# Windowed attention with a gated feed-forward on one core: constants built elsewhere, and a new list for the order of the work

## The chip, the cores and the metric

The kernel runs on one core of a Trainium2 chip. A core has five engines that run beside each other and wait for one another by semaphores: TensorE (PE, matrix products; PEld is its weight load), VectorE (DVE), ScalarE (ACT), GpSimd (POOL) and SyncE (SP), whose queue starts the transfers here. The metric is the device time of one launch in microseconds (us); lower is better.

## The reference

Eight batches, eight heads, 576 positions, 64 per head. Each query sees itself and the 127 positions before it, with a bias that falls with distance by a slope of the head:

```python
scores = scale * np.matmul(q, k.transpose(0, 1, 3, 2))
slopes = 2.0 ** (-8.0 * (np.arange(H) + 1) / H)
mask = (rel >= 0) & (rel < window)             # rel = query position - key position, window = 128
scores = np.where(mask, scores - slopes * np.abs(rel), -1e9)
attn = softmax(scores);  x = attn @ v          # heads side by side: x is (8, 576, 512)
h = gelu(x @ w_in);  u, v = halves of h        # w_in: 512 x 1024
v_n = (v - mean(v)) / sqrt(var(v) + 1e-6) * g_ln
gated = u * (w_sg @ v_n + b_sg)                # w_sg: 576 x 576, over positions
out = x + gated @ w_out
```

## The kernel before

The core works through 32 pairs of heads (pair n is batch n // 4) and, for each batch, the feed-forward part on all 576 positions. A position block is 64 wide (`R`), a tile 128 (`P`). Products of the feed-forward part are made from a high and a low half of every operand (three products for one).

**The order of the work is written out by hand.** Every step has a name and one engine. `ORDER` (line 1141) lists all of them; each engine runs its own steps strictly in the order of the list, and waits at a step until what it needs is there. The steps that matter here, n being the pair, b the batch and t the tile:

- SyncE: `q` load queries and keys, `L` load values, `i` load 128 rows of a weight matrix (0 to 7: `w_in`, 8 to 11: `w_out`), `wl` and `tl` load `w_sg`. The weights come into four buffers with the tag `g`.
- TensorE: `a`, `c` scores of a pair in two parts (`*` is both), `t`, `T` transpose the probabilities (four products each), `z` the first block's, `V` the product with the values, `w` and `v` the gate's part of `x @ w_in` for a tile, `tt` the same for the last 64 positions, `u` the other half of `x @ w_in` (two steps of 12 products for each of four column blocks), `y` the product with `w_sg` (eight steps of 14 products), `O` the product with `w_out`. `W` are idle products on a tile of zeros; they compute nothing that is used. `W0` has 12 of them, `W1` four.
- VectorE: `A`, `B`, `C`, `G` add the bias and take the row's extreme, `R` reciprocal of the sums, `X`, `Y` mask the transposed probabilities on their way out of PSUM, `2` adds up a pair's result, `m`, `b`, `o` and the odd `-` steps split weights into halves, `n..b`, `n..c`, `vn`, `tj`, `tn` normalise the gate (`tn0` is the last such step that batch 0 needs ahead of its `y` steps), `gm` multiplies by the gate, `Us`, `Ul` sums of weights.
- ScalarE: `e`, `E`, `f`, `F`, `j` exponentials, `d`, `H` weight splitting, `P`, `p`, `x`, `h`, `k` copies, `vg`, `tg`, `ug` the gelu, and for the first four pairs the scaling `s`, `r`.
- GpSimd: `S` (and later `s`, `r`) scaling, `+` and the even `-` weight splitting, `l` low halves, `w-`, `t-`, `n..p`.

Ahead of the list stand the constants, lines 85 to 156: an identity for the transposes (`ident`), two triangular masks side by side for both halves of the partitions (`m_both`, used by `X` and `Y`), a selection mask (`sel`, used by `A`) and four bias tables, one for each pair of a batch (`biases`, used by `A` to `G`). They need small temporaries (`ones`, `lo`, `sel_f`, `rel_i`, `rel`), which the kernel before takes from the tag `g`. ScalarE makes the masks' halves and all 16 parts of the bias tables (line 152). In the list before, the `y` steps of batch 0 begin with `y030`.

## Time and profile before

| | before |
|---|---|
| median of 3 runs | 595.48 us (595.41 to 596.38) |
| the profiled execution | 595.18 us |
| its span, first to last instruction | 593.5 us |
| TensorE busy | 567.6 us (96%) |
| VectorE busy | 485.4 us (82%) |
| ScalarE busy | 383.9 us (65%) |
| GpSimd busy | 295.5 us (50%) |

The profile shows one execution. Busy time counts instructions that run, from the start to the end of each. The chain of waits follows the work back from the last instruction, at each step to what released it; its pieces don't overlap, so that they can be added. Two lines of the page, the busy share of TensorE and VectorE in 40 equal slices in tenths, show where the span is not full:

```
PE   6778799799999999999999999999999999999997
DVE  5999898799897978799887896888787989676647
```

### The profile page before, as it was taken

Reading aid. Unit: us, or ns where it says so; the run is one execution under the profiler, and the core shown is the slowest. Engines: PE = TensorE matmul, PEld = TensorE weight load, DVE = VectorE, ACT = ScalarE, POOL = GpSimd, SP = SyncE. Lnnn points to the kernel's source line nnn. Section 1 sums busy time; section 2 is a strip of 40 time slices with the busy share of each in tenths; the row PEclk is TensorE's granted clock in tenths of the full one; section 3 lists DMA queues with packets and bytes.
Section 4 is the critical chain, followed back from the end, with each engine's and each line's share of the span. In section 5 each row is a group of like instructions: output and inputs, shape, how many; then the busy total and the mean of one; then the engine's idle time right before and its main releaser. Section 6 shows DMA issues by size and latency. Waiting matters only on the chain.

```text
span 593.5 us, 14592 instructions
## 1 busy us (share of the span) xinstructions
PE 567.6 (96%) x5495; PEld 513.5 (87%) x5495; DVE 485.4 (82%) x1332; ACT 383.9 (65%) x1085; POOL 295.5 (50%) x283
## 2 busy tenths in 40 slices
...
DVE  5999898799897978799887896888787989676647
...
GB/s 280 172 255 113 150 94 64 7 116 133 121 168 1 200 93 26 183 46 222 164 159 23 140 150 113 122 1 304 113 127 65 37 193 170 2 11 157 127 2 80
DMA packets 43561, 69.78 MB, mean 118 GB/s; under 512 B 3554, under 2 KB 31202, under 8 KB 43492
## 3 DMA queue, kind: packets, MB, share of 16 engines
...
q14 instruction: 26, 0.21, 0.1%
HBM read 56.27 MB, written 12.58 MB: 116 GB/s over the span
## 4 chain that ended last, share of the span: by engine, by line
PE 83%; DVE 11%; ACT 4%; issue 1%; POOL 1%; DVEq 0%; POOLq 0%; ACTq 0%
PE ps_m L602 12%; PE ps_m L1051 12%; PE ps_m L900 11%; PE ps_m L604 11%; PE ps_m L603 11%; PE ps_a L343 4%; PE ps_m L380 3%; PE ps_a L276 3%; PE ps_s L276 3%; PE ps_s L380 3%; DVE e L293 2%; PE ps_m L936 1%; PE ps_m L935 1%; DVE tmp L213 1%; ACT e L309 1%; DVE px L352 1%
## 5 line engine op out<-in xcount | busy, mean ns | idle before, releaser
L330 POOL TENSOR_TENSOR e<-e,rr 128x512 f32<-128x512 f32 (+1 forms) x88 | 78.6, 911 | 127.5 <-DVE rr L321 85.8
L309 ACT ACTIVATE e<-e,stats 128x128 f32<-128x128 f32 (+1 forms) x288 | 110.8, 388 | 15.2 <-DVE stats L293 14.8
L352 DVE TENSOR_TENSOR px<-ps_a,m_both 128x1024 f32<-128x1024 f32 x64 | 77.3, 1213 | 8.5 <-PE ps_a L343 8.5
L602 PE MATMUL ps_m<-ws,region 128*128 128x288 f32 x256 | 78.5, 307 | 0.0
L604 PE MATMUL ps_m<-ws,region 128*128 128x288 f32 x256 | 75.8, 296 | 0.0
L603 PE MATMUL ps_m<-ws,region 128*128 128x288 f32 x256 | 75.7, 296 | 0.0
L725 POOL TENSOR_TENSOR rs<-rs,mhalf 128x1 f32<-128x1 f32 (+1 forms) x40 | 30.7, 769 | 64.5 <-DVE rs L722 60.6
L309 ACT ACTIVATION_READ_ACCUMULATOR e<-e,stats 128x1 f32 x288 | 54.8, 190 | 0.0
L1007 POOL TENSOR_TENSOR region<-u,region 128x576 fp32r<-128x576 f32 x28 | 42.7, 1530 | 23.4 <-ACT region L1001 19.9
L400 POOL TENSOR_TENSOR xs<-xf,xs 128x576 fp32r<-128x576 f32 x32 | 47.0, 1475 | 13.8 <-ACT xs L397 13.8
L1001 ACT ACTIVATE region<-u 128x576 fp32r<-128x576 f32 x35 | 23.8, 685 | 42.8 <-PE ps_m L603 18.7
L343 PE MATMUL ps_a<-ident,e 128*128 128x128 f32 x256 | 40.9, 282 | 9.5 <-issue 3.7
L602 PEld LDWEIGHTS ps_m<-ws,region 128*128 128x128 f32 x256 | 48.4, 189 | 1.6 <-issue 0.8
L604 PEld LDWEIGHTS ps_m<-ws,region 128*128 128x128 f32 x256 | 48.2, 188 | 0.4 <-DVE region L737 0.2
L603 PEld LDWEIGHTS ps_m<-ws,region 128*128 128x128 f32 x256 | 48.3, 189 | 0.1
L602 PE MATMUL ps_m<-wi,xs 128*128 128x512 f32 x112 | 46.8, 418 | 0.0
L603 PE MATMUL ps_m<-wi,xs 128*128 128x512 f32 x112 | 44.3, 395 | 0.0
L604 PE MATMUL ps_m<-wi,xs 128*128 128x512 f32 x112 | 44.2, 395 | 0.0
L343 PEld LDWEIGHTS ps_a<-ident,e 128*128 128x128 f32 x256 | 30.7, 143 | 14.8 <-issue 5.6
L941 DVE TENSOR_TENSOR u<-ps_m,u 128x576 f32<-128x576 f32 x32 | 23.9, 751 | 18.8 <-PE ps_m L936 11.4
L1058 DVE TENSOR_TENSOR xf<-ps_m,xf 128x576 f32<-128x576 f32 x48 | 35.8, 750 | 4.1 <-PE ps_m L1051 3.9
L293 DVE CUSTOM_DVE_ANT_0 e<-ps_s,bias 128x128 f32<-128x128 f32 (+1 forms) x140 | 34.9, 286 | 2.6
(215 smaller groups left out, 1651.3 us busy)
## 6 DMA issues: line engine op xcount, KB each, us to landing
...
```

The lines of the kernel that those rows point to most:

```text
L293: nc.vector.tensor_tensor_reduce(out=dst, in0=src, in1=bs, scale=-1.0 / math.sqrt(D), scalar=3e38, op0=ALU.add, op1=ALU.min, accum_out=acc)
L309: nc.scalar.activation(x, x, AF.Exp, bias=self.nm[0:n, i:i + 1], scale=-1.0, accum_out=self.sm[0:n, i:i + 1])
L330: nc.gpsimd.tensor_tensor(x, y, self.rr[0:n, i:i + k].rearrange("p (m o) -> p m o", o=1).broadcast_to([n, m, c]), ALU.mult)
L343: burst([lambda t=t: nc.tensor.transpose(cv[:, t // 2, t % 2], self.pr[j][:, t, :].rearrange("p (h c) -> p h c", h=2), ident[:, j * R:j * ...
L352: nc.vector.tensor_tensor(xv, cv, mv, ALU.mult)
L400: nc.gpsimd.tensor_tensor(lo_of(self.xs), self.xf, hi_of(self.xs).bitcast(F32), ALU.subtract)
L602: nc.tensor.matmul(dst, ah, bh, start=(first and i == 0), stop=False)
L603: nc.tensor.matmul(dst, ah, bl, start=False, stop=False)
L604: nc.tensor.matmul(dst, al, bh, start=False, stop=(last and i == n - 1))
L900: nc.tensor.matmul(dst, left(n, g, c)[:, ms], right(n, h, c), start=first and c == 0 and k == 0, stop=c == 1 and k == 2, skip_group_check= ...
L1007: engine.tensor_tensor(lo, u(n)[:, fs], hi[:, fs].bitcast(F32), ALU.subtract)
L1051: nc.tensor.matmul(dst, p, q, start=first and f == 0 and k == 0, stop=f == 1 and k == 2, skip_group_check=True)
```

## The change

The constants' temporaries move into one tile with the tag `px`, the buffer in which `X` and `Y` later write the masked probabilities. The four bias tables are made by VectorE, one operation of 128 x 448 each, from a table `rel` in which the slope ratio of the two heads is multiplied in beforehand. `m_both` is cut by four GpSimd selections in place, and the second half of `ident` is copied by GpSimd. The tile of zeros is filled first. With the tag `g` free from the start, the list can place the first loads one behind another. `ORDER` is a new list of the same steps; its idle product ahead of the first scores is `W1` in place of `W0`, and the `y` steps of batch 0 begin with `y000`. Below, the diff of the constants in full, and of the list the part up to the first `y` steps.

```diff
@@ -87,71 +87,59 @@
 
     warm = const.tile([P, 1], F32, name="warm")
     nc.scalar.activation(warm, mhalf, AF.Exp)
-    ident = const.tile([P, P + P // 2], F32, name="ident")
-    make_identity(nc, ident[:, 0:P])
-    nc.vector.tensor_copy(ident[:, P:P + P // 2], ident[:, 0:P // 2])
+    spare = const.tile([P, S2], F32R, name="spare")
+    nc.vector.memset(spare.bitcast(F32), 0.0)
 
 
     def halves(name, n, dt=F32):
         return const.tile([P, n], dt, name=name)
 
-    def twice(x):
-        nc.scalar.copy(x[R:P], x[0:R])
-
-    def temp(name, dt=F32):
-        return mlp.tile([P, P], dt, name=name, tag="g", bufs=NF)[0:R, 0:R]
-
-    ones = temp("ones")
+    setup = att.tile([P, 2 * T * 2 * P], F32, name="setup", tag="px", bufs=1)
+    ones, sel_f, rel_i = [setup[0:R, i * R:(i + 1) * R] for i in range(3)]
+    rel = setup[:, 4 * R:11 * R]
+    low, high = slice(0, R), slice(R, P)
     nc.vector.memset(ones, 1.0)
-
-
-    m_both = halves("m_both", 2 * P)
-    nc.vector.memset(m_both, 1.0)
-    lo = temp("lo")
-    nc.gpsimd.affine_select(out=lo, in_=ones, pattern=[[1, R]], compare_op=ALU.is_ge, fill=0.0, base=0, channel_multiplier=-1)
-    spare = const.tile([P, S2], F32R, name="spare")
-    nc.vector.memset(spare.bitcast(F32), 0.0)
-    for i in range(2):
-        hs = slice(i * R, (i + 1) * R)
-        nc.scalar.activation(m_both[hs, i * R:(i + 1) * R], lo, AF.Copy, scale=-1.0, bias=1.0)
-        nc.scalar.copy(m_both[hs, P + i * R:P + (i + 1) * R], lo)
-
-    sel_f = temp("sel_f")
     nc.gpsimd.affine_select(out=sel_f, in_=ones, pattern=[[1, R]], compare_op=ALU.is_gt, fill=0.0, base=0, channel_multiplier=-1)
-    sel = halves("sel", 4 * R, U8)
-    nc.vector.memset(sel[:, 0:R], 1)
-    for j in range(2):
-        hs = slice(j * R, (j + 1) * R)
-        for i in range(2):
-            nc.scalar.copy(sel[hs, (2 * i + 1) * R:(2 * i + 2) * R], sel_f)
-        nc.scalar.activation(sel[hs, 2 * R:3 * R], sel_f, AF.Copy, scale=-1.0, bias=1.0)
-    sel_first, sel = [sel[:, i * 2 * R:(i + 1) * 2 * R].rearrange("p (t c) -> p t c", t=2) for i in range(2)]
+    nc.gpsimd.iota(rel_i.bitcast(I32), pattern=[[-1, R]], base=0, channel_multiplier=1)
 
 
     slopes = [2.0 ** (-8.0 * (h + 1) / H) for h in range(H)]
     assert all(math.frexp(x)[0] == 0.5 for x in slopes) and D == 4 ** 3
-    rel_i = temp("rel_i", I32)
-    nc.gpsimd.iota(rel_i, pattern=[[-1, R]], base=0, channel_multiplier=1)
-    rel = mlp.tile([P, 4 * R], F32, name="rel", tag="g", bufs=NF)
-    alone, merged, plain = [rel[0:R, i * R:(i + 1) * R] for i in (0, 1, 2)]
-    nc.vector.tensor_copy(merged, rel_i)
+    alone, merged, plain = [rel[low, i * R:(i + 1) * R] for i in (0, 1, 2)]
+    nc.vector.tensor_copy(merged, rel_i.bitcast(I32))
     nc.vector.tensor_scalar(plain, merged, float(R), None, ALU.add)
     nc.vector.scalar_tensor_tensor(out=merged, in0=sel_f, scalar=float(P), in1=merged, op0=ALU.mult, op1=ALU.add)
     nc.vector.scalar_tensor_tensor(out=alone, in0=sel_f, scalar=1e9 / min(slopes), in1=merged, op0=ALU.mult, op1=ALU.add)
-    nc.scalar.copy(rel[0:R, 3 * R:4 * R], merged)
-    nc.scalar.copy(rel[R:P], rel[0:R])
-
+    nc.vector.tensor_copy(rel[low, 3 * R:4 * R], merged)
+    nc.scalar.activation(rel[high, 0:4 * R], rel[low, 0:4 * R], AF.Copy, scale=slopes[1] / slopes[0])
+    nc.scalar.copy(rel[high, 4 * R:7 * R], rel[low, R:4 * R])
+    nc.vector.tensor_scalar(rel[low, 4 * R:7 * R], rel[low, R:4 * R], slopes[1] / slopes[0], None, ALU.mult)
+
+    sel = halves("sel", 4 * R, U8)
+    nc.vector.memset(sel[:, 0:R], 1)
+    for hs in (low, high):
+        nc.scalar.copy(sel[hs].rearrange("p (t c) -> p t c", t=2)[:, :, R:2 * R], over(sel_f, 2))
+        nc.scalar.activation(sel[hs, 2 * R:3 * R], sel_f, AF.Copy, scale=-1.0, bias=1.0)
+    sel_first, sel = [sel[:, i * 2 * R:(i + 1) * 2 * R].rearrange("p (t c) -> p t c", t=2) for i in range(2)]
 
     biases = []
     for hp in range(NPAIR):
         x = halves(f"bias{hp}", 7 * R)
-        for i in range(2):
-            for j in range(2):
-                hs = slice((i ^ j) * R, ((i ^ j) + 1) * R)
-                scale = -slopes[2 * hp + j] * math.sqrt(D)
-                nc.scalar.activation(x[hs, 4 * i * R:(4 + 3 * i) * R], rel[hs, i * R:4 * R], AF.Copy, scale=scale)
+        nc.vector.tensor_scalar(x, rel, -slopes[2 * hp] * math.sqrt(D), None, ALU.mult)
         x = x.rearrange("p (b c) -> p b c", c=R)
         biases.append([x[:, 0:4, :], x[:, 3:7, :]])
+
+    ident = const.tile([P, P + P // 2], F32, name="ident")
+    make_identity(nc, ident[:, 0:P])
+    nc.gpsimd.tensor_copy(ident[:, P:P + P // 2], ident[:, 0:P // 2])
+
+
+    m_both = halves("m_both", 2 * P)
+    nc.gpsimd.memset(m_both, 1.0)
+    for i, hs in enumerate((low, high)):
+        old, own = [m_both[hs, (2 * k + i) * R:(2 * k + i + 1) * R] for k in range(2)]
+        nc.gpsimd.affine_select(out=old, in_=old, pattern=[[-1, R]], compare_op=ALU.is_gt, fill=0.0, base=0, channel_multiplier=1)
+        nc.gpsimd.affine_select(out=own, in_=own, pattern=[[1, R]], compare_op=ALU.is_ge, fill=0.0, base=0, channel_multiplier=-1)
 
     p0s = [const.tile([P, P], F32, name=f"p0_{i}") for i in range(3)]
@@ -1139,85 +1127,85 @@
     ORDER = """
-        q0 i2 q1 W0 a0 c0 A0 B0 W9 W4 W5 a1 c1 W1 i0 i1 wl2 q3 L1 L0 d2 C0 e0 j0 E0 f0 G0 m2 A1 d0 F0 B1 b2 o2 j1 E1
-        R0 m0 C1 b0 o0 G1 s0 e1 f1 F1 t0 X0 S0 +2 +0 R1 T0 Y0 d1 r1 r0 m1 b1 W3 W11 z1 z0 o1 wH2 H0 P0 s1 w-2 +1 a3 A3
-        B3 S1 V0 p0 i3 wl3 q2 tl t1 X1 c3 W8 W7 T1 C3 G3 W2 Y1 i4 a2 A2 B2 e3 E3 wH3 P1 d3 tH H1 F3 d4 j3 V1 f3 x0 E2
-        x1 -0 w-3 t- m3 -1 m4 b3 b4 o4 R3 o3 21 s3 20 t3 X3 c2 C2 +4 S3 +3 L2 i6 i5 L3 i7 q4 q5 i9 G2 r3 d6 h0 p1 e2
-        z3 H2 P3 d5 l0 -2 T3 W10 f2 F2 j2 H3 W6 Y3 V3 x3 p3 m5 b5 m6 b6 o6 R2 23 w00 w20 o5 +6 *5 A5 B5 h1 s2 C5 S2 d7
-        j5 r2 H6 e5 +5 E5 k0 f5 t2 X2 l1 -6 T2 w10 z2 w11 w30 Y2 G5 H5 F5 P2 h3 m7 -3 b7 R5 o7 s5 V2 x2 p2 22 h2 w01
-        a4 t5 w31 -5 A4 B4 X5 +7 l2 S5 l3 c4 w32 T5 w02 v00 v03 w12 C4 G4 d9 E4 j4 e4 H7 f4 F4 k2 -7 m9 b9 R4 o9 Y5 gb
-        L4 L5 i10 q7 i8 q9 s4 r5 S4 r4 t4 z5 w21 w22 vg03 nv30b nv30p vg00 H4 P5 d10 V5 p5 x5 k1 d8 nv00b nv30c m10
-        b10 nv00p -4 +9 X4 T4 v02 z4 v01 25 Y4 nv30h vn03 m8 nv00c P4 vg01 H9 b8 o8 -9 V4 +8 u000 u001 L6 wl1 wH1 wl0
-        nv00h x4 p4 vn00 vg02 k3 wH0 uc00 H8 o10 +10 H10 24 nv20b -10 nv20p *7 A7 nv20c nv10b B7 nv10c nv10p C7 G7 -8
-        u030 tt0 u031 i11 q6 *6 bl q8 L7 e7 nv20h E7 nv10h f7 j7 uc03 F7 vn02 vn01 tj0 R7 A6 B6 u020 u010 tg0 s7 S7 r7
-        t7 C6 nt0b w-1 nt0p w-0 T7 u011 u021 X7 Y7 G6 nt0c z7 E6 d11 bH j6 f6 P7 uc01 V7 nt0h p7 F6 e6 uc02 x7 ug0 m11
-        b11 b- tn0 y030 y031 y020 o11 R6 s6 +11 r6 S6 t6 z6 Us0 X6 gm03 y021 T6 y000 Us1 Us2 27 Y6 y001 gm00 gm02 Us3
...
+        q0 i2 d2 W1 a0 c0 W8 i1 A0 B0 m2 b2 o2 C0 G0 e0 E0 j0 d1 f0 F0 +2 m1 q1 b1 a1 o1 R0 A1 i3 L1 wl2 L0 i0 q3 B1
+        c1 H2 d3 C1 m3 G1 +1 W11 W0 s0 -2 S0 t0 X0 W2 W3 T0 wH2 E1 Y0 f1 j1 r0 W6 z0 F1 e1 P0 w-2 d0 b3 R1 o3 r1 m0 b0
+        o0 V0 W4 z1 a3 A3 B3 s1 wl3 i5 x0 p0 S1 wH3 d5 e3 E3 j3 W5 W10 t1 c3 X1 C3 G3 +0 H0 20 w-3 +3 -0 q2 i6 i4 L3
+        i7 T1 a2 Y1 A2 B2 F3 P1 h0 d6 f3 H1 d4 m5 R3 m6 b5 b6 l0 s3 V1 o6 -1 o5 k0 x1 21 d7 r3 E2 p1 j2 e2 S3 +6 +5 t3
+        W9 X3 m7 b7 m4 c2 C2 G2 z3 W7 T3 w20 w00 w30 P3 h1 l1 f2 F2 Y3 R2 o7 b4 o4 s2 S2 +7 +4 V3 x3 23 i9 gb L2 r2 p3
+        H5 d9 q5 tl q4 wl1 i10 t2 X2 w10 T2 w21 z2 w01 Y2 P2 H7 h3 H3 H4 V2 x2 p2 l3 m9 b9 -5 -7 22 -3 w31 w11 *5 A5
+        B5 wH1 h2 H6 k1 l2 e5 E5 w02 v00 w12 w32 w22 vg00 v01 v02 v03 o9 C5 nv00b nv00c -6 -4 +9 nv00p tH k3 d10 H9
+        nv00h -9 vn00 m10 b10 o10 vg01 vg03 f5 +10 u000 u001 nv30b G5 nv30c nv10b nv30p H10 uc00 j5 nv30h F5 vn03 R5
+        nv10c -10 u030 a4 A4 u031 B4 s5 t5 vg02 nv20b S5 r5 nv10p nv20p w-1 t- X5 c4 C4 e4 uc03 k2 E4 z5 P5 nv10h u020
+        T5 G4 f4 j4 F4 tt0 Y5 nv20c nv20h L5 bl i11 q6 wl0 L4 q7 i8 V5 u021 vn01 R4 vn02 tj0 wH0 p5 x5 tg0 s4 r4 S4
+        w-0 t4 25 X4 nt0b nt0p u010 z4 T4 u011 d11 P4 bH uc01 Y4 nt0c nt0h V4 p4 x4 d8 uc02 ug0 b- tn0 m11 24 m8 b11
+        o11 b8 o8 y000 y001 *7 A7 B7 C7 G7 gm00 +8 +11 j7 H8 H11 Us0 -11 -8 Us1 e7 F7 f7 gh00 E7 y020 y021 y010 Us2
...
```

## Rows read from the trace of the kernel before

**Rows 1.** Busy time by stretch (stretch: us; per engine busy us (x instructions); PEclk, DMA share, GB/s)

```profile
0.00:6.55 6.55, 4.90 (x40) 4.46 (x44) 2.48 (x17) 5.62 (x21) 1.50 (x11) 1.00 0.64 194
6.55:16.00 9.45, 4.99 (x68) 3.73 (x60) 7.05 (x41) 9.40 (x38) 0.10 (x1) 1.00 0.93 322
16.00:74.77 58.77, 46.42 (x510) 33.64 (x510) 53.75 (x165) 49.90 (x166) 38.96 (x32) 0.94 0.54 174
74.77:99.19 24.42, 22.71 (x229) 19.43 (x226) 23.64 (x73) 20.68 (x54) 12.57 (x12) 1.00 0.28 89
99.19:593.50 494.31, 488.58 (x4664) 452.25 (x4661) 398.53 (x1040) 298.33 (x813) 242.37 (x228) 1.00 0.34 107
```

**Rows 2.** Waits of VectorE, 6 to 100 us (us in total, times, longest)

```profile
DVE e L293 <- ACT bias L152: 0.8, 1, 0.8
DVE rr L320 <- ACT e L309: 0.6, 1, 0.6
DVE ps_m L300 <- PE ps_m L276: 0.6, 1, 0.6
```

**Rows 3.** Timeline of ScalarE (start, us, engine, line, operation, out<-in)

```profile
4.83 4.71 ACT L152 ACTIVATE bias<-rel 64x256 f32<-64x256 f32 x16
9.56 0.66 ACT L205 ACTIVATE wst<-wst 128x512 int32<-128x512 uint32 x1
```

**Rows 4.** Chain that ended last, 60 to 130 us (start, us, what)

```profile
68.97 0.66 DVE vg L728
...
70.00 0.43 DVE tmp L211
70.43 1.13 DVE px L352
71.56 0.60 DVE xf L392
...
75.32 0.69 DVE tmp L213
...
80.55 0.21 DVE ps_a L300
...
81.44 1.74 DVE vg L728
...
84.19 0.21 DVE ps_a L300
...
84.93 1.70 DVE vg L728
...
105.11 0.44 PE ps_a L343 x4
...
111.69 1.51 PE ps_s L380 x36
...
115.37 0.81 PE ps_a L276 x18
116.18 0.66 PE ps_s L276 x15
```

**Rows 5.** Timeline of the SyncE queue

```profile
3.06 0.33 SPq L194 DMA_DIRECT2D wst<-w_in  x1
```

**Rows 6.** Busy time by stretch, while the first inputs arrive (columns as in group 1)

```profile
9.30:15.00 5.70, 2.25 (x40) 1.68 (x40) 4.61 (x25) 5.68 (x22) 0.00 (x0) 1.00 0.97 321
```

**Rows 7.** Timeline of VectorE: last v part of batch 0

```profile
100.04 0.75 DVE L737 SCALAR_TENSOR_TENSOR vA<-vg,rs,vA 64x512 fp32r<-64x512 f32 x1
```

**Rows 8.** Timeline of TensorE: first u product, first y product

```profile
74.77 0.40 PE L602 MATMUL ps_m<-xs,wi 128*128 128x288 f32 x1
...
99.19 0.40 PE L602 MATMUL ps_m<-ws,region 128*128 128x288 f32 x1
```

**Rows 9.** The same chain, one run of 288-column products

```profile
186.35 1.60 PE ps_m L1051 x12
```

**Rows 10.** Timeline of GpSimd beside the VectorE operation at 81.44 us

```profile
81.34 1.28 POOL L220 TENSOR_TENSOR wo<-tmp,wo 128x512 fp32r<-128x512 f32 x1 [1.03 <-ACT wo L218]
```

More of the change, by code (lines that the diff above doesn't have):

```diff
@@ new lines, in attention_gmlp @@
+        o11 b8 o8 y000 y001 *7 A7 B7 C7 G7 gm00 +8 +11 j7 H8 H11 Us0 -11 -8 Us1 e7 F7 f7 gh00 E7 y020 y021 y010 Us2
+        gm02 R7 *6 A6 y030 B6 C6 gh02 E6 j6 Uh0 e6 G6 f6 F6 s7 S7 r7 t7 gl02 gl00 X7 T7 y011 z7 y031 Y7 Ul0 R6 gm01
+        gm03 gh01 P7 q9 q8 L7 L6 s6 r6 S6 gl01 V7 gh03 p7 t6 T6 x7 h4 27 X6 Y6 Oa0 gl03 O00 z6 P6 h7 V6 l4 l7 x6 p6
+        oa00 Us3 Us4 26 Us5 h6 h5 l6 l5 O01 *8 u100 A8 B8 C8 G8 Us6 oa01 u101 E8 f8 k5 e8 j8 F8 Uh1 k6 *9 A9 B9 uc10
+        Uh2 E9 k7 j9 e9 u130 R8 Ul1 C9 u131 s8 r8 S8 t8 X8 G9 k4 uc13 f9 z8 P8 F9 u110 T8 Ul2 Y8 tt1 R9 tj1 q10 L9 L8
@@ new lines, in attention_gmlp @@
+        y100 y101 y110 y111 gm10 F11 j11 R11 ks8 l8 ks9 x10 h9 p10 kh3 gm11 kl3 s11 r11 gh11 S11 gl11 y120 y121 t11
+        z11 y130 gm12 gt11 210 X11 y131 gm13 O11 gt13 gh15 gl15 gt12 T11 O15 Y11 oa11 h10 P11 gh12 gh16 gh13 V11 gl12
+        gl16 O16 x11 k8 p11 gh17 oa15 211 oa16 gt14 gl13 gl17 O13 ut25 oa13 O17 *13 O12 oa17 oa12 A13 B13 C13 l10 h11
+        gh14 gl14 O14 oa14 l9 l11 v20 k10 uh25 ul25 k11 vg20 k9 v21 vg21 ut27 ut26 G13 nv02b nv02c j13 nv02p nv02h
+        nv12b nv12p nv12c nv12h vn20 vn21 kd2 kd0 lu22 lu21 tt2 U21 D13 q12 *12 q14 lu20 L13 L12 D12 D11 q15 D10 tj2
```

124 lines of the change are left out of this document (58 added, 66 removed).

## The prediction

> **What bounds the kernel now.** I read the busy time by stretch first. From 99.19 us, where the first `y` product of batch 0 starts, TensorE is busy for 488.58 of 494.31 us; before that, for 4.90 + 4.99 + 46.42 + 22.71 = 79.0 of 99.19 us [rows 1]. So the kernel has two regimes. Behind the first `y` step TensorE sets the end, and both lists hold the same products there. Ahead of it TensorE idles for 20.2 us, and that is what a change to the opening can win. VectorE sets the pace there: 53.75 of the 58.77 us from 16.00 on, then 23.64 of 24.42 us, while in the first two stretches it has 2.48 and 7.05 us of work in 16.0 [rows 1]. Second, VectorE's waits: behind its first scores it lost 0.8 us to the bias tables, 0.6 us to the exponentials and 0.6 us to the second pair's scores [rows 2]. Third, ScalarE's timeline says why: 16 bias operations hold it from 4.83 to 9.54 us, and the first weight split starts only behind them [rows 3].
>
> So the end moves by three things: how early the first `y` step starts, how much TensorE work must stand ahead of it, and how much TensorE waits behind it.
>
> **The change, part by part.**
>
> *Bias tables.* ScalarE loses 4.71 us [rows 3]. VectorE gains four operations of 128 x 448; the nearest row is a tensor_scalar of 128 x 512 at 0.43 us [rows 4], so 1.7 us, between 0 and 7.0 us (each as long as the longest SBUF operation that I read, 1.74 us [rows 4]). They stand ahead of the first `A`, in 6.55 us of which VectorE uses 2.48 [rows 1], and there the price is nothing: the scores come no earlier. Their cover is the wait for the first inputs; were it gone, the 1.7 us would count in full. What is late next is the scores themselves.
>
> The Trainium skill (GPSIMD Engine Reference, section 8, Key points) says that GpSimd shares its SBUF interfaces with VectorE and contends with VectorE instructions in a 2-port mode or with two SBUF inputs. The trace shows the second kind: 1.74 us for an operation that takes 0.66 us alone. If the rule held for the four bias operations, beside the new GpSimd selections, each would stretch as that one did, to 1.1 us and 4.5 us in sum; 2.8 us more would then use up the slack and reach the first `A` by some 1.5 us, and the gain below would be 3.5 instead of 5.0. No row here shows a table build beside a selection.
>
> *Masks, selections, identity.* They leave ScalarE and VectorE for GpSimd, which has 0.10 us of work from 6.55 to 16.00 us [rows 1]; the first transposes come behind that. Price zero; cover gone only if they took over 9 us.
>
> *First loads at once.* The second load goes out at 3.06 us now [rows 5]. Asked for earlier, it can only fill the time up to the arrival of the first inputs: from 9.30 to 15.00 us the transfers already run at a share of 0.97 and 321 GB/s [rows 6]. The second pair's inputs now stand behind one more load of 512 KB, 1.6 us at that rate, and VectorE has three weight steps put ahead of the second pair's `A` to cover it. I take zero, between -1.6 and +1.6 us.
>
> With the tables out of the way VectorE's three early waits, 2.0 us, go. I count 2.0 (bounds: 0, if each is replaced by a wait for a load, and 8.2, all that VectorE idles between 6.55 and 99.19 us: 92.64 - 7.05 - 53.75 - 23.64 [rows 1]).
>
> *The new list.* I counted both lists up to `tn0`, the last VectorE step that the `y` steps need. The new one has 99 VectorE steps there, the old 116; none is added, and 17 have gone behind it: `A`, `B`, `C`, `G` of pairs 6 and 7, `R7`, `X7`, `Y7`, `m8`, `b8`, `o8`, `24`, `m11`, `b11`. In the chain of waits an `A` takes 0.89 us (80.55 to 81.44), a `B`, `C` or `G` 0.74 (84.19 to 84.93), an `X` 1.13, an `m` or `b` 0.43, an `o` 0.69, a `2` step 0.60 [rows 4]. So 2 x 0.89 + 6 x 0.74 + 2 x 1.13 + 4 x 0.43 + 0.69 + 0.60 = 11.5 us (`R7` left out). `tn0` ends at 100.79 us now [rows 7]; less 11.5 and 2.0 that is 87.3 us. The first `y` step started 1.6 us before that end [rows 7, 8], so 85.7 us.
>
> TensorE must be able to follow. Ahead of `u000` the new list has 73 VectorE steps for 89: 16 x 11.5/17 = 10.8 us. `u000` starts at 74.77 us now [rows 8], so at 74.77 - 10.8 - 2.0 = 62.0 us. From there to `y000` stand eight `u` steps of 12 products of 288 columns at 1.60 us a dozen [rows 9], 12.8 us; the tail product `tt0`, eight of 512 columns, 1.9 us by the same rate; the scores of pair 4, 0.81 + 0.66 us; four transposes at 0.44; two value products at 1.51 [rows 4]: 21.0 us, and the first `y` step could start at 83.0 us. VectorE's 85.7 is the later one. The two paths wait for each other at places; I add the 1.7 us that TensorE idles between the same two steps now (24.42 - 22.71 [rows 1]): **87.4 us**.
>
> TensorE has then done less: the scores of pairs 6 and 7 (2 x 1.47), two transposes (0.88) and one value product (1.51) have gone behind the first `y` step, 5.3 us. Gain so far: 99.19 - 87.4 - 5.3 = 6.5 us.
>
> Behind it, the deferred VectorE work must keep up. From `y000` to `V7` TensorE has the eight `y` steps (14 x 0.133 = 1.87 us each), two score pairs and two transposes: 15.0 + 2.9 + 0.9 = 18.8 us. VectorE has 24 steps from `m11` to `Y7`: the 11.5 us above, and `gm00`, `gm02`, `Us0` to `Us2`, `-11`, `o11`, 7 x 0.7 = 4.9 us, together 16.4, and it starts 1.6 us late: 18.0 us. That is level, with the product waiting in between for `gm00` and `gm02`, which free its PSUM: I take 1.5 us of waits (between 0 and 5). **Gain 5.0 us.**
>
> The profiled execution takes 595.18 us, 1.7 more than its span; so 590.2 us. The median of the three runs is 0.3 above it: **590.5 us**. The rest of the list is taken as equal: the waits behind 99.19 us add up to 5.7 us now and may differ by 1.5 either way.
>
> **Rivals.**
>
> *Only the opening counts.* VectorE's deferred steps come back one for one behind the first `y` step; TensorE waits there 3 us more, and what is left are the 2.0 us of early waits: 593.5 us. For it: the balance of 18.8 to 18.0 us has no margin. Against it: TensorE's own later work is the longer from `V7` on.
>
> *More.* All VectorE waits ahead of `tn0` go and TensorE's path sets the start, 83.0 us, without waits behind it: gain 99.19 - 83.0 - 5.3 = 10.9, 584.6 us. Against it: in-order queues on four engines.
>
> *It does not do what it says.* The loads are not earlier, as the transfers are full already [rows 6], ScalarE's freed time goes to waits for them, and the list only swaps waits: 595.5 us.
>
> *Slower, by GpSimd beside VectorE.* At 81.44 us a VectorE operation with two SBUF inputs took 1.74 us, while GpSimd ran one [rows 10]; alone it took 0.66 [rows 4]: 1.1 us. In the new list `o11`, `o8`, `-11`, `Us0` to `Us2` and `Ul0` stand between the first `y` step and `V6`, with 11 GpSimd operations beside them. As the balance has no margin, each stretched one is a TensorE wait. All seven give 7.7 us, against the gain of 6.5: 596.7 us. It decides from the sixth on. Against it: the old list has such pairs too.
>
> **How the numbers follow.** My forecast 0.46 (588 to 592); only the opening 0.22; more 0.12; no change 0.10; slower 0.10. Two kernels that differ by under 0.2% (1.2 us) can't be told apart here. Faster: 0.46 + 0.22 + 0.12 = 0.80; same 0.10; slower 0.10. The range, 585.8 to 594.6 us, leaves out the slower case, most of no change and the far end of more. All chances but the last two have one sign.
>
> **What would show it.** Right: no wait of VectorE for bias tables, the first weight split on ScalarE near 6.5 us, the first `u` product near 62 us, the first `y` product near 87 us, TensorE busy for over 97% from there to 120 us. Wrong: the first `y` product behind 92 us; TensorE waits of more than 3 us for `gm00`, `gm02` or `Y7`; VectorE operations with two SBUF inputs at 1.7 us in a row; or waits of TensorE behind 120 us that the profile of before has not.

## The result, and the profile after

| | before | after |
|---|---|---|
| median, same chip, 4 runs each | 595.93 us (595.41 to 596.85) | 589.73 us (589.52 to 590.10) |
| the profiled execution | 595.18 us | 589.73 us |
| its span | 593.5 us | 588.0 us |
| first `u` product, first `y` product | 74.77, 99.19 us | 62.04, 85.92 us |
| TensorE busy, 5495 products | 567.6 us | 563.6 us |

The ratio (after to before, on the same chip) is 0.9895, with a 95% interval of 0.9878 to 0.9912: faster by 1.05%. On another chip (e9 below) it is 0.9888 [0.9866, 0.9911]. The prediction was 590.5 us in a range of 585.8 to 594.6.

Busy time by stretch of the kernel after, cut where the first scores reach VectorE, at 16 us, at the first `u` and at the first `y` product, as [rows 1] has them for before (stretch, us; per engine busy us and instructions; clock, DMA share, GB/s):

```profile
0.00:6.47 6.47, 2.96 (x28) 2.48 (x32) 3.91 (x20) 3.41 (x9) 2.54 (x16) 1.00 0.68 228
6.47:16.00 9.53, 7.27 (x75) 5.28 (x68) 9.05 (x48) 9.53 (x33) 4.27 (x4) 1.00 1.04 342
16.00:62.04 46.04, 36.31 (x377) 26.69 (x377) 42.83 (x115) 39.33 (x125) 27.97 (x21) 0.96 0.49 157
62.04:85.92 23.88, 22.60 (x238) 20.27 (x238) 22.04 (x62) 21.19 (x55) 14.38 (x15) 1.00 0.38 121
85.92:588.00 502.08, 494.50 (x4785) 456.92 (x4782) 409.84 (x1094) 307.87 (x847) 245.81 (x233) 1.00 0.34 109
```

The difference of the two profiled executions can be read off the last row and that of [rows 1]. The first `y` product comes 99.19 - 85.92 = 13.27 us earlier. Behind it TensorE is busy for 494.50 - 488.58 = 5.92 us more, since that work has moved there, and idles for 7.58 us instead of 5.73, 1.85 more. 13.27 - 5.92 - 1.85 = 5.50 us, the difference of the spans. The medians differ by 6.20 us: the profiled execution of the kernel before (595.18 us) took less than any of its four timed runs. TensorE's busy time falls by 4.0 us in all though it does the same 5495 products; ahead of the first `y` product, where it idles anyway, they took less time, and this is no term of the sum.

What moved the first `y` product is VectorE. From its first scores to that product it is busy for 73.92 us in place of 84.44, 10.52 less, and idles for 5.53 us in place of 8.20, 2.67 less; together 13.19 of the 13.27 us.

ScalarE's timeline answers [rows 3]: the bias operations have gone, and the first weight split starts at 6.06 us instead of 9.56, as soon as its transfer has landed:

```profile
3.89 0.33 ACT L115 COPY setup<-setup 64x192 f32<-64x192 f32 x1
6.06 0.67 ACT L193 ACTIVATE wst<-wst 128x512 int32<-128x512 uint32 x1 [1.83 <-DMA wst<-w_in]
```

VectorE's timeline (start, us; in brackets the idle time ahead and what ended it) shows the tables ahead of the first scores, and `tn0`, which answers [rows 7]:

```profile
4.25 1.30 DVE L128 TENSOR_SCALAR bias<-setup 128x448 f32<-128x448 f32 x4 [0.43 <-ACT setup L115]
6.47 0.30 DVE L288 COPY_PREDICATED ps_s<-sel,ps_s 128x128 f32<-128x128 uint8 x1 [0.92 <-PE ps_s L264]
...
85.97 0.75 DVE L725 SCALAR_TENSOR_TENSOR vA<-vg,rs,vA 64x512 fp32r<-64x512 f32 x1
```

After the four tables VectorE still waits 0.92 us for the scores, so the tables cost nothing there. Its waits from 6 to 100 us, as [rows 2] (us in total, times, longest):

```profile
DVE st L708 <- ACT vg L769: 1.4, 1, 1.4
DVE ps_s L288 <- PE ps_s L264: 0.9, 1, 0.9
DVE region L725 <- ACT region L721: 0.5, 2, 0.3
DVE xf L380 <- PE ps_a L331: 0.5, 1, 0.5
DVE tmp L197 <- ACT tmp L195: 0.5, 1, 0.5
DVE wo L208 <- ACT wo L206: 0.3, 1, 0.3
...
```

The three of [rows 2] are gone, and the wait for the gelu (`vg`), which [rows 2] leaves out, is 1.4 us instead of 2.6 in the kernel before:

```profile
DVE st L720 <- ACT vg L781: 2.6, 1, 2.6
```

New ones have come, 2.0 us in all: 0.8 for ScalarE's weight splits (`tmp`, `wo`), 1.0 at `region` and `xf`, and 0.2 for the gelu of the last 64 positions. TensorE's timeline answers [rows 8]:

```profile
62.04 0.40 PE L590 MATMUL ps_m<-xs,wi 128*128 128x288 f32 x1 [1.09 <-ACT vg L769]
...
85.66 0.33 PE L372 MATMUL ps_a<-p,vt 64*64 64x64 f32 x4
85.92 0.40 PE L590 MATMUL ps_m<-ws,region 128*128 128x288 f32 x1
```

The first `y` product follows the last value product without a gap. Behind it, the same kind of windows:

```profile
85.92:105.00 19.08, 19.08 (x195) 18.07 (x193) 18.01 (x67) 16.25 (x49) 8.99 (x8) 1.00 0.32 98
105.00:200.00 95.00, 94.28 (x933) 85.39 (x932) 82.10 (x211) 54.48 (x148) 41.09 (x39) 1.00 0.34 114
200.00:350.00 150.00, 148.61 (x1525) 136.02 (x1524) 127.31 (x378) 103.83 (x308) 81.38 (x79) 1.00 0.39 127
350.00:400.00 50.00, 48.90 (x510) 46.01 (x509) 40.60 (x111) 28.93 (x84) 23.65 (x23) 1.00 0.28 92
400.00:575.00 175.00, 174.85 (x1569) 163.12 (x1568) 132.62 (x320) 102.66 (x258) 85.16 (x82) 1.00 0.31 99
575.00:588.00 13.00, 8.78 (x64) 8.31 (x63) 9.20 (x12) 1.72 (x3) 5.54 (x4) 1.00 0.27 91
```

Two rows of the same view of the kernel before:

```profile
350.00:400.00 50.00, 50.00 (x518) 47.50 (x517) 39.80 (x123) 34.10 (x94) 22.65 (x26) 1.00 0.23 70
...
580.50:593.50 13.00, 9.37 (x68) 8.81 (x66) 8.93 (x13) 2.21 (x4) 5.84 (x4) 1.00 0.27 91
```

To 105 us, where I had put 1.5 us of waits, TensorE has no idle time at all (19.08 of 19.08). The idle time is later: 0.72, 1.39, 1.10, 0.15 and, at the end, 4.22 us.

### The profile page after: what moved, and what is told of

It reads as the page before. It is cut to its first block, busy times and chain, and to the rows that moved or that the text cites. A ratio compares the mean times of both kernels' runs of the same rounds, so it can differ in the third digit from the quotient of the medians.

```text
span 588.0 us, 14571 instructions
## 1 busy us (share of the span) xinstructions
PE 563.6 (96%) x5495; PEld 511.6 (87%) x5495; DVE 487.7 (83%) x1336; ACT 381.3 (65%) x1066; POOL 295.0 (50%) x288
## 4 chain that ended last, share of the span: by engine, by line
PE 82%; DVE 12%; POOL 2%; issue 2%; ACT 1%; DMA 1%; DVEq 0%; POOLq 0%; ACTq 0%
PE ps_m L590 12%; PE ps_m L1039 11%; PE ps_m L592 11%; PE ps_m L591 11%; PE ps_m L888 11%; PE ps_a L331 4%; PE ps_a L264 3%; PE ps_s L264 3%; PE ps_m L368 3%; PE ps_s L368 3%; DVE e L281 2%; DVE u L999 2%; PE ps_m L924 1%; PE ps_m L923 1%; DVE px L340 1%
## 5 line engine op out<-in xcount | busy, mean ns | idle before, releaser
L318 POOL TENSOR_TENSOR e<-e,rr 128x512 f32<-128x512 f32 (+1 forms) x88 | 76.3, 886 | 96.3 <-DVE rr L309 87.8
L995 POOL TENSOR_TENSOR region<-u,region 128x576 fp32r<-128x576 f32 x28 | 44.1, 1580 | 21.9 <-ACT region L989 17.4
L850 POOL TENSOR_TENSOR region<-u,region 128x576 fp32r<-128x576 f32 x18 | 27.3, 1516 | 27.3 <-ACT region L844 15.3
L331 PE MATMUL ps_a<-ident,e 128*128 128x128 f32 x256 | 38.9, 278 | 2.0 <-DVE stats L281 0.9
L1039 PE MATMUL ps_m<-region,sum 128*128 128x288 f32 x252 | 36.8, 299 | 1.4 <-DVE region L995 1.1
```

The costliest lines, as they stand in the source:

```text
L318: nc.gpsimd.tensor_tensor(x, y, self.rr[0:n, i:i + k].rearrange("p (m o) -> p m o", o=1).broadcast_to([n, m, c]), ALU.mult)
L331: burst([lambda t=t: nc.tensor.transpose(cv[:, t // 2, t % 2], self.pr[j][:, t, :].rearrange("p (h c) -> p h c", h=2), ident[:, j * R:j * ...
L995: engine.tensor_tensor(lo, u(n)[:, fs], hi[:, fs].bitcast(F32), ALU.subtract)
L1039: nc.tensor.matmul(dst, p, q, start=first and f == 0 and k == 0, stop=f == 1 and k == 2, skip_group_check=True)
```

## The experiments

Each is the kernel after with the edit shown, if nothing else is said, and was timed beside the kernel before on its own chip. As the chips differ by some 0.2%, I compare ratios between groups. e1 to e4 shared a chip, e5 to e8 another, e9 to e12 a third. My theory: the list gives most of it, by deferring VectorE work behind the first `y` product; the constants give the early waits of VectorE. The rivals: the opening gives it all, or the early requests of the loads do, or something behind the first `y` product.

**e1, the new constants alone**

```diff
     ORDER = """
-        q0 i2 d2 W1 a0 c0 W8 i1 A0 B0 m2 b2 o2 C0 G0 e0 E0 j0 d1 f0 F0 +2 m1 q1 b1 a1 o1 R0 A1 i3 L1 wl2 L0 i0 q3 B1
+        q0 i2 q1 W0 a0 c0 A0 B0 W9 W4 W5 a1 c1 W1 i0 i1 wl2 q3 L1 L0 d2 C0 e0 j0 E0 f0 G0 m2 A1 d0 F0 B1 b2 o2 j1 E1
...
```

> The new constants with the old list. Theory A (two parts that add up: the opening's waits and the new list): the bias tables and the first loads take some 2 us of waits off VectorE, the list's share is missing, so the first y product stands near 97 us and the time is 593.3 to 594.0 us. Rival B (the list is everything): 595.5 to 596 us. Rival C (the constants are everything): 589.5 to 590.5 us.

Measured: 595.28 us, ratio 0.9977 [0.9965, 0.9989], 1.4 us (0.7 to 2.1). The first `y` product comes at 97.55 us, 1.64 earlier. VectorE's three waits of [rows 2] are gone, but a new one of 1.0 us has come at 25 us:

```profile
25.19 1.22 DVE L340 TENSOR_TENSOR px<-ps_a,m_both 128x1024 f32<-128x1024 f32 x1 [1.03 <-PE ps_a L331]
```

It ends as the transposes do, and they ran late: the granted clock (before the DMA share) had read below 1.00 since 10 us. TensorE had been busy for 0.04 us from 12 to 14 us, and from 14 to 16 us the clock read 0.50.

```profile
10.00:15.00 5.00, 2.32 (x24) 1.55 (x17) 4.76 (x25) 5.00 (x22) 1.53 (x2) 0.84 0.92 304
15.00:20.00 5.00, 2.66 (x13) 2.27 (x12) 4.93 (x11) 4.17 (x16) 2.25 (x2) 0.82 0.48 145
20.00:25.00 5.00, 4.70 (x65) 4.23 (x65) 3.91 (x15) 2.72 (x11) 4.19 (x4) 0.66 0.71 210
```

Behind the first `y` product TensorE idles for 7.09 us here, 1.36 more than in the kernel before, 1.1 of it in one wait for ScalarE's `u`, which e10 has too. So this one trace keeps little of the earlier start (its span is 593.4 us); the gain of 1.4 us rests on the times alone.

**e2, the new list alone**: the constants of the kernel before, the list of the kernel after.

```diff
-        nc.vector.tensor_scalar(x, rel, -slopes[2 * hp] * math.sqrt(D), None, ALU.mult)
+        for i in range(2):
+            for j in range(2):
+                hs = slice((i ^ j) * R, ((i ^ j) + 1) * R)
+                scale = -slopes[2 * hp + j] * math.sqrt(D)
+                nc.scalar.activation(x[hs, 4 * i * R:(4 + 3 * i) * R], rel[hs, i * R:4 * R], AF.Copy, scale=scale)
...
```

> The old constants with the new list. Theory A: the new list asks for the first weight split (d2, m2) ahead of C0, but ScalarE is at the bias tables until 9.5 us, so VectorE stalls some 2 to 3 us behind B0, and the rest of the list's gain is kept: 592 to 593 us, first y product near 89 us. Rival B: 589.5 to 590.2 us. Rival C: 595.5 us or more.

Measured: 592.46 us, ratio 0.9929 [0.9914, 0.9944], 4.2 us (3.3 to 5.1); the first `y` product at 88.62 us. VectorE now waits for the late tables and, behind them, the late split:

```profile
DVE tmp L209 <- ACT tmp L207: 2.1, 2, 1.6
...
DVE e L293 <- ACT bias L152: 0.9, 1, 0.9
```

So the list carries 4.2 of the 6.3 us (0.0105 of 595.93), and "only the opening" falls. The parts add up to 5.6 of 6.3 (each with an interval of some 1 us): most of the gain is a sum of the two, and whether the rest is more than chance stays open. The expectation held: 592 to 593 us and a first `y` product near 89.

**e3, the bias tables back on ScalarE**, in 16 parts, the new list and the rest as they are

```diff
-        nc.vector.tensor_scalar(x, rel, -slopes[2 * hp] * math.sqrt(D), None, ALU.mult)
+        for hs in (low, high):
+            for cs in (slice(0, 4 * R), slice(4 * R, 7 * R)):
+                nc.scalar.activation(x[hs, cs], rel[hs, cs], AF.Copy, scale=-slopes[2 * hp] * math.sqrt(D))
```

> The changed kernel, only the bias tables again by ScalarE in 16 parts (4.7 us). Theory A: the first weight split starts at 8.6 us instead of 6.06 and ends at 9.8, VectorE stands still from 8.1 to 9.8 us ahead of m2, and as VectorE sets the start of the first y product, all of it arrives: 1.5 to 2 us more than the changed kernel, 591.2 to 591.8 us. Rival (VectorE has slack ahead of the first y product that takes it up): within 0.5 us of the changed kernel.

Measured: 594.03 us, ratio 0.9946 [0.9927, 0.9965]: 0.0051 or 3.0 us are lost, not the 1.5 to 2 of the expectation. The six runs lie apart, though: two at 592.03 and 592.24 us, 1.5 to 1.7 us behind the 590.5 that the kernel after would take on this chip (0.9895 of 596.81), one at 593.33, and three from 594.73 to 594.90, 4.2 to 4.4 behind. The profiled execution is the one of 594.90 us. VectorE's timeline there shows two pairs of waits:

```profile
8.19 0.29 DVE L283 CUSTOM_DVE_ANT_0 e<-ps_s,bias 128x128 f32<-128x128 f32 x1 [0.46 <-ACT bias L130]
10.49 0.43 DVE L199 TENSOR_SCALAR tmp<-tmp 128x512 f32<-128x512 f32 x1 [1.79 <-ACT tmp L197]
22.30 1.23 DVE L342 TENSOR_TENSOR px<-ps_a,m_both 128x1024 f32<-128x1024 f32 x1 [1.20 <-PE ps_a L333]
...
28.31 0.30 DVE L290 COPY_PREDICATED ps_s<-sel,ps_s 128x128 f32<-128x128 uint8 x1 [1.21 <-PE ps_s L266]
```

The first two, 2.25 us, are the tables and the split behind them. The other two, 2.4 us, are for TensorE, which from 20 to 25 us ran at the lower of its two levels (1.2 GHz) the whole time, after it had been busy for 2.78 of 5 us:

```profile
15.00:20.00 5.00, 2.78 (x15) 1.78 (x14) 4.79 (x27) 5.00 (x17) 4.60 (x4) 0.90 0.76 262
20.00:25.00 5.00, 4.89 (x35) 4.55 (x39) 3.59 (x7) 3.55 (x15) 1.15 (x2) 0.50 0.61 209
```

The first pair alone would about fit the two shortest times (and e2, 592.46 us, which has these stalls too), both pairs the three longest; but only one run has a trace, so that the second pair is not shown to be what parts them.

**e4, the temporaries in the tag `g` again**, so that the second load can't be asked for at once

```diff
-    setup = att.tile([P, 2 * T * 2 * P], F32, name="setup", tag="px", bufs=1)
-    ones, sel_f, rel_i = [setup[0:R, i * R:(i + 1) * R] for i in range(3)]
-    rel = setup[:, 4 * R:11 * R]
+    ones, sel_f, rel_i = [mlp.tile([P, P], F32, name=x, tag="g", bufs=NF)[0:R, 0:R] for x in ("ones", "sel_f", "rel_i")]
+    rel = mlp.tile([P, 7 * R], F32, name="rel", tag="g", bufs=NF)
```

> The changed kernel, only the temporaries back in the weights' buffers, so that the first loads wait for them. Theory A: the transfers are full from 5 to 15 us anyway; the first weights come 0.5 to 1 us later and VectorE has A0 and B0 to do meanwhile, so 589.7 to 590.4 us, no more than 0.6 us behind the changed kernel. Rival (the early requests are what lets the list put the weight split first): VectorE stalls for m2 and m1, 591 us or more.

Measured: 590.21 us, ratio 0.9887 [0.9869, 0.9904], as the kernel after. In SyncE's timeline the first weight loads go out at 2.47 us; with the temporaries elsewhere (second fence, the kernel after) at 1.25:

```profile
2.47 0.81 SPq L181 DMA_DIRECT2D wst<-w_in  x2
```

```profile
1.25 0.89 SPq L182 DMA_DIRECT2D wst<-w_in  x2
```

The times show nothing for these 1.2 us, as expected: the ratios differ by -0.5 us, with some 1.5 us either way. The one trace, of the longest of the four runs (590.86 us), has the first `y` product at 86.91 us, 1.0 later. So the buffer's move is not shown to be a part of the gain, and up to 1 us of it stays possible.

**e5, the new list only as far as the first `y` step of batch 1**, then the steps that are left in the old list's order

```diff
...
-        y100 y101 y110 y111 gm10 F11 j11 R11 ks8 l8 ks9 x10 h9 p10 kh3
+        y100 F11 q14 kd0 j11 y110 y101 y111 ks8 ks9 R11 gm10 s11 h9 p10
...
```

> The changed kernel, its list only up to y100 (some 140 us), then the steps that are left in the order of the old list. Theory A (the opening's gain is complete by the first y product; the new list gives 1.9 us back later, in waits at 140 to 250 us, 350 to 400 us and in the tail): 1.0 to 1.9 us faster than the changed kernel, 587.8 to 588.7 us. Rival (the gaps belong to work that was moved behind the first y product and come anyway, or the seam makes new ones): 589.5 us or more.

Measured: 590.67 us, ratio 0.9884 [0.9868, 0.9901], 6.9 us: the whole gain. The 1.0 to 1.9 us better of theory A did not come: 0.0011 or 0.7 us, with intervals that overlap. In the trace TensorE idles for 6.86 us behind the first `y` product (at 87.25 us), 0.7 less than in the kernel after. What the new list changes behind that step gives nothing that these runs can tell from zero.

**e6 and e7, eight idle VectorE operations** (memsets of 128 x 288) ahead of `nt0b`, which belongs to the first `y` step's inputs, and behind the first `y` step ahead of pair 7's `A`

```diff
+    idle = const.tile([P, S2], F32, name="idle")
+    def more_vector():
+        for _ in range(8):
+            nc.vector.memset(idle, 0.0)
+    add("more", "DVE", 2.0, 0.0, more_vector)
...
-        25 X4 nt0b nt0p u010
+        25 X4 more nt0b nt0p u010
...
```

In e7 the same `more` stands in `y001 *7 more A7` instead.

> The changed kernel with eight extra memsets of 128x288 on VectorE (some 2.2 us, they touch nothing else) ahead of the normalisation of the tail in batch 0. Theory A (VectorE sets the start of the first y product): the first y product near 88 us and 2.0 to 2.4 us more than the changed kernel, 591.7 to 592.1 us. Rival (TensorE or ScalarE sets it): within 0.6 us of the changed kernel.

> The changed kernel with the same eight memsets on VectorE behind tn0, ahead of A7. In the changed kernel Y7 ends 1.5 us ahead of V7 and the first gm step ends 0.5 us ahead of the y step that needs its buffer. Theory A (level, as predicted, with a small margin): TensorE waits 0.7 to 1.7 us, 590.4 to 591.4 us. Rival (VectorE has slack behind the first y product): within 0.4 us of the changed kernel.

Measured: 594.64 us, 0.9949 [0.9934, 0.9964], and 594.61 us, 0.9951 [0.9937, 0.9965]. Each costs 3.2 to 3.3 us against the kernel after (0.0054 and 0.0056, with some 1.3 us either way), more than either theory A said; the eight took 3.27 us in either place, and not the 2.2 that I had assumed. First e6, then e7, in TensorE's timeline:

```profile
87.59 2.61 PE L368 MATMUL ps_s<-px,vt 64*64 64x192 f32 x32 [2.67 <-DVE px L340]
```

```profile
98.29 0.58 PE L590 MATMUL ps_m<-ws,region 128*128 128x288 f32 x1 [2.73 <-DVE u L929]
```

In e6 a value product (`V4`) waits for VectorE's masks, and the first `y` product comes at 90.19 us. In e7 the first `y` product stands at 86.18, and a later one waits 2.73 us for `gm`, which frees its PSUM. So VectorE is the bound on both sides as soon as more than a small margin is put in: 3.27 - 2.67 = 0.6 us ahead of the first `y` product and 3.27 - 2.73 = 0.5 us behind it.

The wait is not all that is lost. Behind it TensorE's clock falls to the lower of its two levels (0.50 from 98.20 to 100.00 us in e7): one `y` step of 14 products and the change to the next work take 3.49 us in e7 and 1.96 in the kernel after, 1.53 more. First the kernel after, then e7 (columns as above, the clock before the DMA share):

```profile
95.14:97.10 1.96, 1.96 (x17) 1.80 (x15) 1.93 (x4) 1.96 (x9) 0.00 (x0) 1.00 0.00 0
```

```profile
98.29:101.78 3.49, 3.49 (x15) 3.32 (x15) 3.31 (x7) 2.50 (x10) 0.00 (x0) 0.54 0.00 0
```

In e6 the same: the 2.60 us behind the wait read 0.50, and the kernel after passes that place in 1.62. So the traces lose 4.0 us ahead of the first `y` product in e6 (against e7 on the same chip) and 4.26 behind it in e7; the spans, 592.7 and 592.8 us, are 4.7 and 4.8 above that of the kernel after. The times by the ratios say less, within their interval.

**e8, one product in each idle TensorE step**

```diff
-    IDLE = [(12, "ps_a"), (4, "ps_a"), (4, "ps_s"), (4, "ps_s"), (4, "ps_a"), (4, "ps_m"), (4, "ps_m"), (3, "ps_m"), (4, "ps_m"), (4, "ps_m"), (2, "ps_m"), (2, "ps_m")]
+    IDLE = [(1, "ps_a"), (1, "ps_a"), (1, "ps_s"), (1, "ps_s"), (1, "ps_a"), (1, "ps_m"), (1, "ps_m"), (1, "ps_m"), (1, "ps_m"), (1, "ps_m"), (1, "ps_m"), (1, "ps_m")]
```

> The changed kernel with one idle product in each of the twelve W steps instead of 2 to 12 (51 in all before). Theory D (the granted clock of TensorE matters in the opening, through VectorE steps that wait for transposes and scores): the clock falls to its lower level for some microseconds between 10 and 30 us, VectorE waits for TensorE there by 1 to 3 us, and the time is 591 to 592.5 us. Rival (idle products are free, and so is the clock, as TensorE has slack): 589.2 to 590.0 us.

Measured: 592.03 us, ratio 0.9902 [0.9885, 0.9920]; by its median 0.0007 to 0.0014 behind the kernel after, with intervals that overlap. The trace is plainer: the clock reads 0.57, 0.50 and 0.50 in the three stretches from 10 to 25 us, VectorE waits 2.8 us for scores (its first wait of 0.7 included; 0.9 in the kernel after), and the first `y` product comes at 87.99 us, 2.1 later. Behind it this execution takes 502.0 us, the kernel after 502.1, so that nothing of it is given back. That is theory D by time and trace, though the intervals don't exclude a smaller loss.

**e9, the kernel after again**, as the anchor of the last group

> The changed kernel once more, beside the three others of this group, so that they have it on their own chip. Expected: 0.9895 of the kernel before, as in its first timing (0.9878 to 0.9912), some 590.5 us if this chip is the slower one; first y product at 85.9 us, and 1.1 us of TensorE waits between 350 and 400 us and 1.1 at the last gate product again. If these two waits are elsewhere, they belong to the execution and not to the list.

Measured: 590.30 us, ratio 0.9888 [0.9866, 0.9911]. The first `y` product comes at 86.02 us, and TensorE's idle time lies in the same places (1.09 us from 350 to 400, 4.17 behind 575), so these waits belong to the list.

**e10, as e1, with `W0` and `W1` exchanged**

```diff
-        q0 i2 q1 W0 a0 c0 A0 B0 W9 W4 W5 a1 c1 W1 i0 i1 wl2 q3 L1 L0 d2 C0 e0 j0 E0 f0 G0 m2 A1 d0 F0 B1 b2 o2 j1 E1
+        q0 i2 q1 W1 a0 c0 A0 B0 W9 W4 W5 a1 c1 W0 i0 i1 wl2 q3 L1 L0 d2 C0 e0 j0 E0 f0 G0 m2 A1 d0 F0 B1 b2 o2 j1 E1
```

> The new constants with the old list, in which only the two idle TensorE steps change places: W1 (4 products) ahead of the first scores, W0 (12) ahead of the first transposes. Theory A (the constants' own part came out at 1.4 us instead of 2.0 because TensorE idled from 11 to 14 us and its granted clock then read 0.50 to 0.86, so that VectorE waited 1.4 us for scores and 1.0 for masks' input): the granted clock between 14 and 25 us above 0.9, these waits under 1 us together, the first y product near 96.5 us (97.55 with the old place), and 0.9960 to 0.9970 of the kernel before in place of 0.9977. Rival B (those waits are the old list's order and not the clock): the clock higher, but the first y product at 97.5 us or later and the ratio at 0.9977 or above, since the dozen idle products stand ahead of the transposes.

Measured: 596.05 us, ratio 0.9989 [0.9975, 1.0003], first `y` product at 98.33 us. Theory A fails here: the low clock only came later. Between 20 and 25 us it read 0.66 again, after TensorE had been busy for 1.96 of 5 (and from 30 to 40 us 0.67 and 0.50):

```profile
15.00:20.00 5.00, 1.96 (x14) 1.51 (x13) 4.90 (x11) 4.16 (x18) 2.85 (x3) 1.00 0.41 113
20.00:25.00 5.00, 4.43 (x63) 3.85 (x64) 4.53 (x16) 3.00 (x11) 3.58 (x3) 0.66 0.66 221
```

The first `y` product and the ratio are as rival B has them. In the old list a dozen idle products don't cure the low clock.

**e11, the same exchange in the kernel after**

```diff
-        q0 i2 d2 W1 a0 c0 W8 i1 A0 B0 m2 b2 o2 C0 G0 e0 E0 j0 d1 f0 F0 +2 m1 q1 b1 a1 o1 R0 A1 i3 L1 wl2 L0 i0 q3 B1
+        q0 i2 d2 W0 a0 c0 W8 i1 A0 B0 m2 b2 o2 C0 G0 e0 E0 j0 d1 f0 F0 +2 m1 q1 b1 a1 o1 R0 A1 i3 L1 wl2 L0 i0 q3 B1
...
-        c1 H2 d3 C1 m3 G1 +1 W11 W0 s0 -2 S0 t0 X0 W2 W3 T0 wH2 E1 Y0 f1 j1 r0 W6 z0 F1 e1 P0 w-2 d0 b3 R1 o3 r1 m0 b0
+        c1 H2 d3 C1 m3 G1 +1 W11 W1 s0 -2 S0 t0 X0 W2 W3 T0 wH2 E1 Y0 f1 j1 r0 W6 z0 F1 e1 P0 w-2 d0 b3 R1 o3 r1 m0 b0
```

> The changed kernel, in which only the two idle TensorE steps change places again, as the list before has them: W0 (12 products) ahead of the first scores, W1 (4) ahead of the first transposes. Theory A (the dozen ahead of the first transposes holds the clock): the granted clock falls to 0.5 to 0.8 somewhere between 10 and 25 us, VectorE waits 1 us or more for scores or transposes there, the first y product 0.7 to 2 us behind 85.9, and 0.3 to 1.2 us more than the changed kernel beside it. Rival B (the clock early on costs nothing, the list's other steps do it): the first y product within 0.5 us of 85.9 us and the time within 0.1% of the changed kernel.

Measured: 591.24 us, ratio 0.9902 [0.9881, 0.9924], 0.9 us behind e9 on the same chip, with intervals that overlap; the first `y` product at 88.30 us, 2.3 later. First e9, then e11:

```profile
10.00:15.00 5.00, 4.63 (x48) 4.12 (x49) 4.69 (x28) 5.00 (x17) 3.16 (x3) 0.66 1.07 321
15.00:20.00 5.00, 3.66 (x29) 3.02 (x27) 4.71 (x13) 4.48 (x22) 2.91 (x3) 1.00 0.64 222
20.00:25.00 5.00, 4.74 (x70) 3.96 (x71) 4.70 (x16) 5.00 (x15) 2.58 (x3) 1.00 0.54 169
```

```profile
10.00:15.00 5.00, 4.83 (x46) 3.64 (x41) 4.72 (x27) 5.00 (x17) 3.15 (x3) 0.66 1.10 344
15.00:20.00 5.00, 3.31 (x15) 2.93 (x16) 3.73 (x13) 4.07 (x20) 3.03 (x3) 0.70 0.53 179
20.00:25.00 5.00, 4.85 (x50) 4.17 (x48) 4.39 (x8) 3.81 (x11) 1.50 (x2) 0.62 0.49 184
```

To 15 us the two are alike. With the dozen ahead of the transposes the clock is back at its upper level (2.4 GHz) from 15 us; without it VectorE's busy time in the two stretches falls by 1.3 us. This trace is as theory A has it, though it is of the longest of the six runs (592.33 us); the time agrees in sign only. Five more executions have the opening of the kernel after: its first profile, e6, e7 and e12 read 1.00 in both later stretches, but e5 read 0.77 and 0.89, with its first `y` product at 87.25 us. So a part of the 2.3 us may be chance of the one execution. The mean granted clock over the whole span points the same way as theory A in every run: 0.986 to 0.988 in the six of e11, 0.990 to 0.994 in the five of e9.

**e12, the new list up to the scores of pair 14**, then the old one's order for what is left

```diff
...
-        y211 y200 212 X13 y201 *14 gm21 gm20 A14 B14 C14 y220 T13 y221 G14
+        y211 y200 212 X13 y201 *14 A14 B14 T13 C14 G14 gm21 y220 j14 F14
...
```

> The new list up to the scores of pair 14, near 250 us, and behind them the steps that are left in the order of the old list; new constants. Theory A (behind the first y product the new list keeps TensorE 1.9 us longer idle than the old, by waits at 350 to 400 us and at the end): the first y product at 86 us, the wait of 1.1 us at 350 to 400 and that of 1.1 at the last gate product gone, 0.75 us at 450 to 500 us come in with the old list, 0.7 us less than the changed kernel in sum, 0.1%. Rival B (no difference): within 0.05% of it, the waits only elsewhere. It is also the best version that I can put together from the two lists.

Measured: 593.56 us, ratio 0.9945 [0.9925, 0.9965], 3.3 us behind e9, where a tenth of a per cent better was expected. The start is the same (first `y` product at 85.90 us), but the seam adds a wait:

```profile
238.25 0.40 PE L590 MATMUL ps_m<-ws,region 128*128 128x288 f32 x1 [2.21 <-DVE u L929]
```

I had read where each list's waits were and spliced between them, and there theory A held: TensorE has no idle time from 350 to 400 us, and 0.75 us of it from 450 to 500. But at the seam the old list puts `A14` to `G14` ahead of `gm21`, and `y220` waits for `gm21`. It is e7 once more, 140 us later, with a lower clock behind it (0.67 over the next 3.55 us): this `y` step and a pair's scores take 5.07 us, in the kernel after 3.50. With a wait of 0.56 us just ahead, at a transpose, the seam costs 2.21 + 0.56 + 1.57 = 4.3 us, and the span is 3.6 above that of e9. No version here is shown to beat the kernel after: e4 and e5 have its time within the intervals.

## Why the prediction was right

It forecast the time, the mechanism and the two main marks in the trace. By its own steps:

- **Bias tables hidden: right, smaller.** 1.30 us for four, not 1.7, behind which VectorE still waits 0.92 us. GpSimd's last selection began at 2.81 us and the copy of the identity at 3.12 (0.24 us), while the tables start at 4.25 us. So the rule of the Trainium skill on shared interfaces (GPSIMD Engine Reference, section 8, Key points) had no chance to act: no run here shows a table beside a selection.
- **First loads at once, zero: right** as far as the times of e4 tell, with up to 1 us open.
- **Early waits, 2.0 us: right in size, with a reserve.** All three go, as do 0.5 us for scores and 1.2 of the 2.6 for the gelu, while 2.0 us of new waits come in; with the gaps too short to be listed VectorE idles for 2.67 us less. By themselves the constants gave 1.4 us (e1), and e10 0.7 (-0.2 to 1.5). What was missing in the step is TensorE: new waits of VectorE for transposes and scores, behind stretches at a lowered clock.
- **The list, `u000` at 62.0, `tn0`'s end at 87.3: right.** 62.04 and 86.72 us. Moving 17 VectorE steps at the prices of [rows 4] was the right sum, 11.5 us forecast against 10.52 less ahead of the first `y` product and 11.31 more behind it; and e6 shows that this work sets the start: 3.27 us put back delayed it by 4.0.
- **First `y` product at 87.4: 1.5 us too late.** The term that was off is the 1.7 us added to VectorE's 85.7 for mutual waits. TensorE did idle between the two products (23.88 - 22.60 = 1.28 us, 1.12 of it for ScalarE's `u` at 66.61 us), but inside its own path, which held 22.60 us of work instead of the 21.0 that I had summed. So the mutual waits belonged to the 83.0. Nor was VectorE's path the later one, by 2.7 us, as I had it. In the kernel after, the chain that ended last runs on TensorE from 66.61 us to the first `y` product, but for two VectorE steps:

```profile
80.20 0.69 DVE xf L380
80.89 1.14 DVE px L340
```

  The two paths end level, VectorE with 0.6 us to spare at `V4` (e6) and 0.9 at `tn0`, which ends at 86.72 us and is first read at 87.63. That VectorE's 85.7 lies within 0.2 us of the measured 85.92 is luck: `tn0` ended 0.6 us earlier than forecast, and the product started 0.8 us ahead of that end and not 1.6.
- **TensorE work moved behind it, 5.3: 5.92.** So 7.35 us are won so far, and not 6.5.
- **Waits behind it, 1.5 at `gm00`, `gm02` or `Y7`: the wrong place, near in size.** There TensorE idles 0.00 us; the margin that I called absent is 0.5 us (e7). The loss is 1.85 us and later, in particular 1.1 us between 350 and 400 us (none in the kernel before), and 4.22 instead of 3.63 us in the last 13 us. TensorE's longest waits behind 85.92 us in the kernel after:

```profile
PE ps_m L1039 <- DVE region L995: 1.1, 2, 0.7
PE ps_m L888 <- issue: 1.1, 1, 1.1
PE ps_a L331 <- DVE stats L281: 0.9, 1, 0.9
...
```

  The second is not new (0.9 us in the kernel before); the third lies between 350 and 400 us, and 0.7 of the first at the last gate product. Waits behind 120 us that the profile of before has not were on my list of signs of being wrong. They came; I had allowed them as 1.5 either way and put no term in. The errors, 0.85 won and 0.35 lost, leave 5.5 us in place of 5.0: they partly cancel, and that the measured median lies 0.8 us from the forecast owes something to it.
- **Rivals.** "Only the opening" falls with e2, "more" because TensorE's path took 23.88 us from `u000` and not 21.0, "doesn't do what it says" with the first split at 6.06 us. For the slower case, VectorE lost no time to GpSimd that TensorE noticed: 19.08 of 19.08 us busy from the first `y` product on. (The 0.66 us of [rows 4] that I called alone had a GpSimd operation of 128 x 1 beside it.)
